# Linear attention and a silu feed-forward on one core: which queue issues the loads and the DMA transposes, in which order, and from which buffers

## The chip, the cores and the metric

The kernel runs on one core of a Trainium2 chip. The core has five engines with their own in-order instruction streams: PE (TensorE, matrix multiply into PSUM), DVE (VectorE), ACT (ScalarE), POOL (GpSimd) and SP (SyncE), and 16 DMA engines that move data. SP computes nothing; it issues transfers. Any stream that issues a transfer is held for the time of the issue, and an instruction that waits holds all that stand behind it in its stream. The metric is the device time in microseconds (us), the median of several runs.

## The reference

The inputs are q, k, v of shape (4 batches, 8 heads, 768 positions, 64), a decay `lam` per head, and two weights, (512, 2048) and (2048, 512), all float32. First comes linear attention with decay, in blocks of 64 positions, with a 64 x 64 state per batch and head:

```python
for b in range(nb):
    intra = (qb @ kb^T * Dmask) @ vb             # Dmask[i,j] = lam^(i-j) for i >= j, else 0
    inter = (qb * lam^(pos+1)) @ kv_state
    out[b] = intra + inter
    kv_state = lam^64 * kv_state + (kb * lam^(63-pos))^T @ vb
```

The heads of one position are then put side by side, which gives x with 3072 rows of 512, and the result is `silu(x @ w_in) @ w_out`, 3072 x 512 in float32.

## The kernel before, in words

**Tiling.** The 3072 rows are 24 chunks of 128 positions, six to a batch. Heads go in pairs: a pair's two 64-wide heads fill the 128 partitions. The decay is put into q and v by two tables (`tab`, from Ln and Exp of `lam` in `c_tab`, lines 235 to 246), so the mask is a plain 0/1 one. For each chunk:

- `prep_q` (L353, once for two chunks) multiplies q by its table into `qb` (L371, POOL; the first queries also on DVE) and transposes it to `qT`.
- `prep_k` (L411) casts K to bf16 into `kbd` (L424), block-diagonal over the pair, with zeros set once beforehand, and transposes it to `kT`.
- `prep_v` (L454) multiplies V by its table into `vs` (L468, POOL) and copies that block-diagonally into `vbd` (L475, DVE).
- `attn` (L483) makes scores `sc` (L536) and masks them into `ss` (L542), sums the output `op` from scores and state (L565), adds to the state `kv` in PSUM (L585) and copies the state out as bf16 `sbd` (L599, L601). The output becomes `x` (L615, L617).

For chunks 0 to 7 (`NPET = 8`) the transposes are done on PE into PSUM tiles of tag `o`, and copied out (L387 to L400, L435 to L443). From chunk 8 on they are DMA transposes from one SBUF tile into another, issued on SP's queue (L406 for q, L448 for k).

**Feed-forward.** Chunks are gathered into groups of 2, 2, 2, 2, 4, 4, 4, 4 (`GROUPS`). `ffn1` (L626) makes 128 rows of the hidden layer at a time into PSUM `h` (L633), and ACT applies silu into `g` (L640). `ffn2` (L646) sums 16 such pieces into PSUM `o` (L656) for each chunk; ACT or DVE copies it to `ob` (L666), and SP stores it (L673).

**Loads.** K and V of chunks 0 to 3 come as two transfers of 128 KB each (`load_kvh`, L285 and L288, buffers `kfh` and `vfh`). All later K and V come in segments of 4 to 8 blocks of 64 positions (`SEGS`), one transfer per head, so eight per segment and tensor (`load_seg`, L303, two buffers `kf`, two `vf`). q comes in 512 KB (`load_q`, L275, two buffers). The weights come in float32 (`load_w`, L324, five buffers `wt`) and are cast into their places (L335, L337). Everything is issued by SP, in the order in which the program lists the loads (lines 680 to 708).

**What sets the order of work.** Nothing is written down by hand. Each step is an `Op` with its possible engines and an assumed duration, what it depends on, and the buffers it takes and uses. `plan` (L46) simulates the engines: it takes again and again the operation that can start earliest, ties going to the lower priority number, and gives it its engine. A buffer tag has `SLOTS[tag]` buffers; an operation that takes a new one waits in the plan for all users of the one that it replaces, and buffers of a tag must be taken in order, but for tag `o`. `FREE` is when each engine is assumed to begin, `SEEN` the delay until others see a result. A transfer is assumed to begin 1.3 us after its issue or when DMA is free, to move `bytes / rate`, and to be seen 0.7 us later; no more than eight are under way. The loads are a chain, each after the one before. The instructions are then emitted in the order of the planned starts, so each engine's stream, SP's too, has the order of this simulation:

```python
def load(fn, nbytes, ndesc, rate, deps=(), alloc=(), uses=(), prio=None):      # L262
    o = add(fn, ("SP", max(420.0, 60 + 1.05 * ndesc)), ..., after=chain[-1:])
```

Up to 26 us (`WARM`) gaps of PE in the plan are filled with multiplications by zero (L737).

Of the kernel before, what the change touches and what calls it, by code (L numbers as in the profile page):

```python
# [42 lines left out]
FREE = {"PE": 900.0, "DVE": 2400.0, "ACT": 900.0, "POOL": 3300.0, "SP": 900.0}  # L43


def plan(ops, slots):  # L46
    free = dict(FREE)
    dma_free = 0.0
    landed = []
    given = {t: [] for t in slots}  # L50
    for i, op in enumerate(ops):
        op.n = i
    todo = list(ops)
    order = []
    while todo:
        best = None
        for op in todo:
            ready = op.at
            ok = True
            for d in op.after:  # L60
                if d.start is None:
                    ok = False
                    break
                ready = max(ready, d.start)
            if not ok:
                continue
            for d in op.deps:
                if d.start is None:
                    ok = False
                    break  # L70
                if d.seen > ready and not (len(op.opts) == 1 and d.eng == op.opts[0][0] == "PE"):
                    ready = d.seen
            if not ok:
                continue
            for b in op.alloc:
                if b.tag != "o" and b.idx != len(given[b.tag]):
                    ok = False
                    break
                k = len(given[b.tag]) - slots[b.tag]
                if k >= 0:  # L80
                    for u in given[b.tag][k].users:
                        if u.start is None:
                            ok = False
                            break
                        if u.seen > ready:
                            ready = u.seen
                if not ok:
                    break
            if not ok:
                continue  # L90
            if op.bytes and len(landed) >= 8:
                ready = max(ready, landed[-8])
            for e, dur in op.opts:
                s = max(free[e], ready)
                key = (s, op.prio, s + dur)
                if best is None or key < best[0]:
                    best = (key, op, e, s, dur)
        if best is None:
            for op in todo[:40]:
                print(op.n, op.fn.__qualname__, op.prio, [d.n for d in op.deps + op.after if d.start is None],  # L100
                      [(b.tag, b.idx, len(given[b.tag])) for b in op.alloc])
        assert best is not None, "no operation can go on"
        _, op, e, s, dur = best
        op.start, op.eng, op.end = s, e, s + dur
        free[e] = s + dur
        if op.bytes:
            t = max(op.end + 1300.0, dma_free)
            dma_free = t + op.bytes / op.rate
            op.seen = dma_free + 700.0
            landed.append(op.seen)  # L110
        else:
            op.seen = op.end + SEEN[e]
        for b in op.alloc:
            given[b.tag].append(b)
        todo.remove(op)
        order.append(op)
    order.sort(key=lambda o: (o.start, o.n))
    return order
# [19 lines left out]
def kernel(  # L138
# [23 lines left out]
    SLOTS = {"qf": 2, "qb": 2, "qT": 3, "kf": 2, "vf": 2, "kfh": 2, "vfh": 2, "kbd": 3, "kT": 3, "vs": 3, "vbd": 3,  # L162
             "ss": 3, "sbd": 3, "x": 3, "g": 24, "ob": 3, "wt": 5, "sc": 1, "op": 1, "kv": 1, "h": 3, "o": 2}
# [61 lines left out]
    nc.vector.memset(zk[0], 0.0)  # L225
    nc.vector.memset(zv[0], 0.0)
    nc.vector.memset(zs[0], 0.0)
    late_zero = [zk[1], zv[1], zs[1], zk[2], zv[2], zs[2]]
# [33 lines left out]
    def load(fn, nbytes, ndesc, rate, deps=(), alloc=(), uses=(), prio=None):  # L262
        nload[0] += 1
        p = nload[0] if prio is None else prio
        o = add(fn, ("SP", max(420.0, 60 + 1.05 * ndesc)), deps=deps, alloc=alloc, uses=uses,
                nbytes=nbytes, rate=rate, prio=p, after=chain[-1:])
        chain.append(o)
        return o

    def load_q(b, j):  # L270
        t = Buf("qf")

        def f():
            new(t, [128, H, 2, D], F32)
            nc.sync.dma_start(out=t.tile, in_=q[b, :, 256 * j:256 * j + 256, :].rearrange("h (s t) d -> s h t d", t=2))  # L275
        o = load(f, 524288, 1024, 330.0, alloc=[t])
        return t, [o]

    def load_kvh(src, tag, b, c):
# [7 lines left out]
        def f1():  # L287
            nc.sync.dma_start(out=t.tile[64:128], in_=r[1])  # L288
        a = load(f0, 131072, 256, 330.0, alloc=[t])
        z = load(f1, 131072, 256, 330.0, uses=[t])  # L290
        return t, [a, z]

    def load_seg(src, tag, b, c0, n):
        t = Buf(tag)
        last = []
        for hh in range(8):
# [7 lines left out]
            o = load(f, 64 * n * 256, 64 * n, 222.0, alloc=[t] if hh == 0 else [], uses=[] if hh == 0 else [t])  # L304
            last.append(o)
# [4 lines left out]
    def load_w(which, i, n):  # L310

        t = Buf("wt")
# [12 lines left out]
        o = load(f, 524288 * n, 512 if which == "in" else 256 * n, 386.0, alloc=[t])  # L325
# [27 lines left out]
    def prep_q(b, j, head):  # L353
# [9 lines left out]
        prep = []  # L363
        for i in range(nn):
            sl = slice(2 // nn * i, 2 // nn * (i + 1))

            def f(e, i=i, sl=sl):
                if i == 0:
                    new(tb, [128, 2, H, D], BF16)
                eng = nc.gpsimd if e == "POOL" else nc.vector  # L370
                eng.tensor_tensor(tb.tile[:, sl], tf.tile.rearrange("p h s d -> p s h d")[:, sl],  # L371
                                  tabq[:, j, sl, :, None].to_broadcast([128, 2 // nn, H, D]), op=AL.mult)
            opts = [("POOL", pool_ns(1024 // nn))] + ([("DVE", dve_ns(512))] if head else [])
            prep.append(add(f, opts, deps=list(o) + [o_tab], after=prep, alloc=[tb] if i == 0 else [],
                            uses=[tf] + ([tb] if i else []), prio=pr(c)))
        if c < NPET:
            ps = Buf("o")
            tr = []
            for i in range(nn):
                sl = range(2 // nn * i, 2 // nn * (i + 1))  # L380

                def ft(i=i, sl=sl):
                    if i == 0:
                        new(ps, [128, 2, NP, 128], BF16)
                    for s in sl:
                        for p in range(NP):
# [4 lines left out]
            for i in range(nn):  # L391
                sl = slice(2 // nn * i, 2 // nn * (i + 1))

                def fe(e, i=i, sl=sl):
                    if i == 0:
                        new(tq, [128, 2, NP, 128], BF16)
                    if e == "ACT":
                        nc.scalar.activation(tq.tile[:, sl], ps.tile[:, sl], AF.Copy)
                    else:
                        nc.vector.tensor_copy(tq.tile[:, sl], ps.tile[:, sl])  # L400
                z.append(add(fe, [("DVE", dve_ns(1024 // nn, 2)), ("ACT", act_ns(1024 // nn))], deps=[tr[i]], after=z,
                             alloc=[tq] if i == 0 else [], uses=[ps] + ([tq] if i else []), prio=pr(c)))
        else:
            def fx():
                new(tq, [128, 2, NP, 128], BF16)
                nc.sync.dma_start_transpose(out=tq.tile.rearrange("a s p b -> a (s p) b"),  # L406
                                            in_=tb.tile.rearrange("a s h d -> a (s h d)"))
            z = [add(fx, ("SP", 700.0), deps=prep, alloc=[tq], uses=[tb], nbytes=262144, rate=200.0, prio=-50)]
        qT[b, j] = (tq, z)

    def prep_k(c, src, src_ops, coff, head):  # L411
# [16 lines left out]
        if c < NPET:  # L428
            ps = Buf("o")
# [15 lines left out]
        else:  # L445
            def fx():
                new(tk, [128, 2, NP, 128], BF16)
                nc.sync.dma_start_transpose(out=tk.tile.rearrange("a s p b -> a (s p) b"),  # L448
                                            in_=kb.tile.rearrange("a s p h d -> a (s p h d)"))
            z = add(fx, ("SP", 700.0), deps=prep, alloc=[tk], uses=[kb], nbytes=262144, rate=200.0, prio=-50)  # L450
# [3 lines left out]
    def prep_v(c, src, src_ops, coff, head):  # L454
# [14 lines left out]
        a = add(f, [("POOL", pool_ns(512))] + ([("DVE", dve_ns(512))] if head else []), deps=list(src_ops) + [o_tab], alloc=[tv], uses=[src], prio=pr(c))  # L469
# [153 lines left out]
    gts = {}  # L623
    PF = 1000.0

    def ffn1(g, m):  # L626
        n = C * GROUPS[g]
        hb, gb = Buf("h"), Buf("g")
# [9 lines left out]
        def fe():  # L638
            new(gb, [128, n], BF16, padded=[128, 512])
            nc.scalar.activation(gb.tile, hb.tile, AF.Silu)  # L640
        z = add(fe, ("ACT", act_ns(n)), deps=[a], alloc=[gb], uses=[hb], prio=-30)
        gts[g, m] = (gb, z)
# [3 lines left out]
    def ffn2(g, mt):  # L646
        po = Buf("o")
        prev = None
        for kk in range(4):
            ms = range(4 * kk, 4 * kk + 4)  # L650

            def f(kk=kk, ms=ms):
                if kk == 0:
                    new(po, [128, DM], F32)
                for m in ms:
                    nc.tensor.matmul(po.tile, lhsT=gts[g, m][0].tile[:, mt * C:(mt + 1) * C], rhs=w_out_bf[:, m, :],  # L656
# [3 lines left out]
                       uses=([] if kk == 0 else [po]) + [gts[g, m][0] for m in ms], prio=PF + 100 * g + 20 + 4 * mt + kk)  # L660
# [13 lines left out]
        add(fd, ("SP", 420.0), deps=[z], uses=[bo], nbytes=262144, rate=386.0, prio=-40)  # L674
# [6 lines left out]
    loaded_q[0, 0] = load_q(0, 0)  # L681
# [8 lines left out]
    loaded_q[0, 1] = load_q(0, 1)  # L690
# [3 lines left out]
    for i in range(4, 8):  # L694
        load_w("in", i, 1)
    for i in range(0, 8, 2):
        load_w("out", i, 2)
    loaded_q[0, 2] = load_q(0, 2)
    for i, (b, c0, n) in enumerate(SEGS):
        seg_k[i] = load_seg(k, "kf", b, c0, n)  # L700
        seg_v[i] = load_seg(v, "vf", b, c0, n)
        for j in range(3):
            if (b, j) not in loaded_q and 4 * j + 4 <= c0 + n + 2:
                loaded_q[b, j] = load_q(b, j)
    for b in range(B):
# [4 lines left out]
    zero_ops = [add(lambda t=t: nc.gpsimd.memset(t, 0.0), ("POOL", 1100.0), prio=-70 + 20 * (i > 2)) for i, t in enumerate(late_zero)]  # L710
# [23 lines left out]
    for op in plan(ops, SLOTS):  # L734
# [6 lines left out]
        if "e" in op.fn.__code__.co_varnames[:op.fn.__code__.co_argcount]:  # L741
# [33 lines left out]
```

## Time and profile before

| | |
|---|---|
| median of 3 runs | 251.68 us (250.38 to 253.49) |
| the profiled execution's own time | 250.55 us |
| its span in the profile | 248.8 us |
| mean granted clock of PE | 0.977 |
| PE busy | 214.9 us, 86% |
| ACT, DVE, POOL busy | 119.4, 108.5, 52.7 us |
| bytes read from HBM, written | 27.27 MB, 6.29 MB |
| all bytes of the DMA queues | 40.15 MB, 161 GB/s over the span |
| first L633 (feed-forward) on PE | 19.75 us |
| last L565 (attention) on PE | 188.0 us |

How to read it: the span is cut into stages by what PE does. Until about 20 us it has the first two chunks' attention and zero multiplications; then feed-forward and attention alternate; from 190 us the last feed-forward groups alone are left, with PE never idle until the last copy and store. "Busy" of PE includes the zero multiplications (11.3 us). A wait "A <- B: 68.1, 5, 18.0" says that A waited for B 68.1 us in total, five times, 18.0 us at the longest; idle time of an engine that nobody waits for costs nothing. The queue of SP as an issuer is written SPq.

### The profile page before, as it was taken

Reading aid. Unit: us, or ns where it says so; the run is one execution under the profiler, and the core shown is the slowest. Engines: PE = TensorE matmul, PEld = TensorE weight load, DVE = VectorE, ACT = ScalarE, POOL = GpSimd, SP = SyncE. Lnnn points to the kernel's source line nnn. Section 1 sums busy time; section 2 is a strip of 40 time slices with the busy share of each in tenths; the row PEclk is TensorE's granted clock in tenths of the full one; section 3 lists DMA queues with packets and bytes.
Section 4 is the critical chain, followed back from the end, with each engine's and each line's share of the span. In section 5 each row is a group of like instructions: output and inputs, shape, how many; then the busy total and the mean of one; then the engine's idle time right before and its main releaser. Section 6 shows DMA issues by size and latency. Waiting matters only on the chain.

```text
span 248.8 us, 4537 instructions
## 1 busy us (share of the span) xinstructions
PE 214.9 (86%) x1781; PEld 126.3 (51%) x1781; DVE 108.5 (44%) x197; ACT 119.4 (48%) x230; POOL 52.7 (21%) x58
## 2 busy tenths in 40 slices
PE   6679899969599699566999896995899999999994
PEld 4477776735397386322455352443454444444441
DVE  4884852447286846594177247255740000000000
ACT  2369776723166287421685233654434751177310
POOL 7802100330320910180061005504300000000000
PEclk9999999997889999997999999999999999999999
DMA  5999999544698998699767989979442001210022
GB/s 143 243 281 251 358 383 328 140 125 91 178 243 190 251 216 154 127 285 211 148 161 162 167 192 237 217 156 191 80 122 84 0 0 45 84 42 0 5 82 84
DMA packets 94885, 40.15 MB, mean 161 GB/s; under 512 B 69264, under 2 KB 89744, under 8 KB 94864
## 3 DMA queue, kind: packets, MB, share of 16 engines
q1 hardware_dynamic: 94720, 39.86, 68.1%
q8 instruction: 14, 0.23, 0.4%
q14 instruction: 7, 0.06, 0.1%
q10 hardware_dynamic: 144, 0.00, 0.0%
HBM read 27.27 MB, written 6.29 MB: 135 GB/s over the span
## 4 chain that ended last, share of the span: by engine, by line
PE 48%; DMA 19%; SPq 15%; DVE 9%; issue 3%; POOL 2%; ACT 2%; POOLq 0%; DVEq 0%; ACTq 0%
PE h L633 22%; PE o L656 19%; SPq L303 10%; DMA qf<-in_q_dram 8%; DVE vbd L475 5%; DMA vf<-in_v_dram 3%; DMA wt<-in_moe_w_in_dram 3%; PE op L565 3%; DMA kfh<-in_k_dram 2%; DMA qT<-qb 2%; PE kv L737 2%; DVE sbd L601 1%; POOL vs L468 1%; DMA kf<-in_k_dram 1%; DVE ss L542 1%
## 5 line engine op out<-in xcount | busy, mean ns | idle before, releaser
L633 PE MATMUL h<-x,w_in_bf 128*128 128x256 bf16 (+1 forms) x512 | 92.8, 333 | 0.4 <-ACT g L640 0.4
L656 PE MATMUL o<-w_out_bf,g 128*128 128x512 bf16 x384 | 90.3, 383 | 0.0
L640 ACT ACTIVATE g<-h 128x256 bf16<-128x256 f32 (+1 forms) x128 | 62.0, 490 | 35.8 <-PE h L633 34.0
L633 PEld LDWEIGHTS <-w_in_bf 128*128 128x128 bf16 x512 | 48.9, 99 | 32.9 <-issue 2.2
L656 PEld LDWEIGHTS <-g 128*128 128x128 bf16 x384 | 35.7, 99 | 37.3 <-issue 1.1
L468 POOL TENSOR_TENSOR vs<-vf,tab 128x512 bf16<-128x512 f32 x20 | 20.8, 1062 | 86.4 <-DMA vf<-in_v_dram 68.1
L475 DVE COPY vbd<-vs 64x512 bf16<-64x512 bf16 x48 | 29.6, 617 | 19.5 <-POOL vs L468 18.8
L666 ACT ACTIVATE ob<-o 128x512 f32<-128x512 f32 x24 | 14.3, 597 | 44.6 <-PE o L656 43.5
L371 POOL TENSOR_TENSOR qb<-qf,tab 128x1024 bf16<-128x1024 f32 (+1 forms) x12 | 22.3, 1856 | 34.5 <-DMA qf<-in_q_dram 34.4
L585 PE MATMUL kv<-vs,kbd 128*128 128x64 bf16 x176 | 12.1, 196 | 17.9 <-POOL vs L468 8.9
L599 ACT ACTIVATE sbd<-kv 64x256 bf16<-64x256 f32 x42 | 15.8, 376 | 23.5 <-PE kv L585 18.9
L424 DVE CAST kbd<-kf 64x512 bf16<-64x512 f32 x40 | 19.4, 486 | 16.1 <-DMA kf<-in_k_dram 15.3
L585 PEld LDWEIGHTS <-kbd 128*128 128x128 bf16 x176 | 10.2, 100 | 26.3 <-issue 16.9
L542 DVE TENSOR_TENSOR ss<-sc,mask 128x512 bf16<-128x512 f32 x20 | 13.8, 691 | 16.0 <-PE sc L536 15.6
L601 DVE CAST sbd<-kv 64x256 bf16<-64x256 f32 x38 | 16.0, 422 | 7.9 <-PE kv L585 3.4
L565 PE MATMUL op<-ss,vbd 128*128 128x64 bf16 (+1 forms) x192 | 15.3, 198 | 1.3 <-DVE ss L542 1.0
L615 ACT ACTIVATE x<-op 128x512 bf16<-128x512 f32 x16 | 11.9, 746 | 8.5 <-PE op L565 8.4
L737 PE MATMUL kv<-zt 128*128 128x256 bf16 x69 | 11.3, 319 | 3.7 <-ACT sbd L599 2.1
L565 PE MATMUL op<-qT,sbd 128*128 128x64 bf16 (+1 forms) x160 | 14.4, 196 | 0.0
L565 PEld LDWEIGHTS <-vbd 128*128 128x128 bf16 x192 | 12.8, 99 | 2.5 <-DVE vbd L475 0.6
L565 PEld LDWEIGHTS <-sbd 128*128 128x128 bf16 x160 | 11.5, 99 | 2.7 <-issue 1.3
L536 PE MATMUL sc<-qT,kT 128*128 128x64 bf16 x160 | 7.9, 193 | 4.7 <-DMA kT<-kbd 3.0
(52 smaller groups left out, 94.5 us busy)
## 6 DMA issues: line engine op xcount, KB each, us to landing
qf<-in_q_dram SPq DMA_DIRECT2D x12, 512.0 KB, 5.2
out_dram<-ob SPq DMA_DIRECT2D x24, 256.0 KB, 2.4
wt<-in_moe_w_in_dram SPq DMA_DIRECT2D x8, 512.0 KB, 7.0
wt<-in_moe_w_out_dram SPq DMA_DIRECT2D x4, 1024.0 KB, 10.0
kf<-in_k_dram SPq DMA_DIRECT2D x32, 96.0 KB, 3.0
vf<-in_v_dram SPq DMA_DIRECT2D x32, 96.0 KB, 2.8
kfh<-in_k_dram SPq DMA_DIRECT2D x8, 128.0 KB, 5.6
vfh<-in_v_dram SPq DMA_DIRECT2D x8, 128.0 KB, 5.6
```

Of the source, the lines that this page charges most:

```text
L303: nc.sync.dma_start(out=t.tile[64 * two:64 * two + 64, :, p, :], in_=r)
L371: eng.tensor_tensor(tb.tile[:, sl], tf.tile.rearrange("p h s d -> p s h d")[:, sl], tabq[:, j, sl, :, None].to_broadcast([128, 2 // nn, H, ...
L424: nc.vector.tensor_copy(kb.tile[hs, :, :, h, :], i)
L468: eng.tensor_tensor(tv.tile, i, t[:, :, :, None].to_broadcast([128, 2, NP, D]), op=AL.mult)
L475: nc.vector.tensor_copy(vb.tile[hs, :, :, h, :], tv.tile[hs])
L542: nc.vector.tensor_tensor(sb.tile.rearrange("a s p b -> a (s p) b"), ps.tile.rearrange("a s p b -> a (s p) b"), mask1[:, None].rearrange(" ...
L565: nc.tensor.matmul(o_cols(p, sub), lhsT=l, rhs=r, start=not ovs["started"], stop=i == len(steps) - 1, skip_group_check=True)
L585: nc.tensor.matmul(kvp.tile[:, p, :], lhsT=kb.tile[:, s, p, :, :], rhs=tv.tile[:, s, p, :], start=st, stop=True, skip_group_check=True)
L601: nc.vector.tensor_copy(nb.tile[hs, :, h, :], kvp.tile[hs])
L633: nc.tensor.matmul(hb.tile, lhsT=w_in_bf[:, ko, m * 128:(m + 1) * 128], rhs=xt[g].tile[:, ko, :], start=(ko == 0), stop=(ko == 3))
L640: nc.scalar.activation(gb.tile, hb.tile, AF.Silu)
L656: nc.tensor.matmul(po.tile, lhsT=gts[g, m][0].tile[:, mt * C:(mt + 1) * C], rhs=w_out_bf[:, m, :], start=(m == 0), stop=(m == 15))
```

## The change

- **First loads.** The second halves of each `load_kvh` and of the first two q loads (heads 4 to 7) are issued by ACT, the first halves by SP. The two products of a head's `prep_q` are split by heads in place of by position parity, each waits for its own half, and both are on DVE.
- **Transposes.** Both DMA transposes are issued by ACT in place of SP. PE's transposes of chunks 0 to 7, which there were before, take PSUM tiles of tag `h` (three) in place of `o` (two).
- **Loads and buffers.** K and V segments and weights share seven buffers `big` (before: 2 `kf`, 2 `vf`, 5 `wt`, of the same size); q has four buffers in place of two. `SEGS` stays as it is. The last four `w_in` loads become two of 1 MB. The last two `w_out` loads come after the first segment, and each batch's q before the segments that need it.
- **g.** With 256 columns, two pieces of the hidden layer share one `g` buffer, so 24 buffers hold twice as many of them.
- **Zeroing.** The block-diagonal tiles are all zeroed on DVE; before, those of the second and third buffers were zeroed on POOL. V products of chunks 2 and 3 no longer may go to DVE.
- **The planner.** Assumed issue times are constants (620, 650, 660, 400, 560 ns; 1280 for a transpose), rates are lower, loads are planned no more than 5 us ahead of DMA once it is booked past 40 us, and after 60 us results are assumed to be seen 0.4 us later, transfers 3 us later.

```diff
-FREE = {"PE": 900.0, "DVE": 2400.0, "ACT": 900.0, "POOL": 3300.0, "SP": 900.0}
+FREE = {"PE": 900.0, "DVE": 2600.0, "ACT": 1200.0, "POOL": 5000.0, "SP": 800.0}
+LATE = 60000.0
+DEPTH = 5000.0
...
-                if b.tag != "o" and b.idx != len(given[b.tag]):
+                if b.tag not in ("o", "h") and b.idx != len(given[b.tag]):
...
+            if op.bytes and op.prio > 0.0 and dma_free > LATE - 20000.0:
+                ready = max(ready, dma_free - DEPTH)
...
+        if op.bytes and op.rate == 170.0:
+            dma_free = max(op.end + 1300.0, dma_free) + op.bytes / op.rate
+            op.seen = op.end + 2000.0 + 2.0 * op.bytes / op.rate
...
+            if op.start > LATE:
+                op.seen += 3000.0
         else:
-            op.seen = op.end + SEEN[e]
+            op.seen = op.end + SEEN[e] + (400.0 if op.start > LATE else 0.0)
...
-    SLOTS = {"qf": 2, ..., "kf": 2, "vf": 2, ..., "wt": 5, ...}
+    SLOTS = {"qf": 4, ..., "big": 7, ...}
...
-    def load(fn, nbytes, ndesc, rate, deps=(), alloc=(), uses=(), prio=None):
+    def load(fn, nbytes, issue, rate, alloc=(), uses=(), eng="SP"):
...
-        def f1():
-            nc.sync.dma_start(out=t.tile[64:128], in_=r[1])
+        def f1():
+            nc.scalar.dma_start(out=t.tile[64:128], in_=r[1])
...
-                nc.sync.dma_start_transpose(out=tq.tile.rearrange("a s p b -> a (s p) b"),
+                nc.scalar.dma_start_transpose(out=tq.tile.rearrange("a s p b -> a (s p) b"),
...
-            z = [add(fx, ("SP", 700.0), deps=prep, alloc=[tq], uses=[tb], nbytes=262144, rate=200.0, prio=-50)]
+            z = [add(fx, ("ACT", 1280.0), deps=prep, alloc=[tq], uses=[tb], nbytes=262144, rate=170.0, prio=-50)]
...
+        half = n == 256 and m % 2
+        gb = gts[g, m - 1][0] if half else Buf("g")
...
-    loaded_q[0, 0] = load_q(0, 0)
+    loaded_q[0, 0] = load_q(0, 0, ("SP", "ACT"))
...
-    for i in range(4, 8):
-        load_w("in", i, 1)
-    for i in range(0, 8, 2):
-        load_w("out", i, 2)
-    loaded_q[0, 2] = load_q(0, 2)
+    load_w("in", 4, 2)
+    load_w("in", 6, 2)
+    load_w("out", 0, 2)
+    load_w("out", 2, 2)
     for i, (b, c0, n) in enumerate(SEGS):
-        seg_k[i] = load_seg(k, "kf", b, c0, n)
-        seg_v[i] = load_seg(v, "vf", b, c0, n)
         for j in range(3):
-            if (b, j) not in loaded_q and 4 * j + 4 <= c0 + n + 2:
+            if 4 * j < c0 + n and (b, j) not in loaded_q:
                 loaded_q[b, j] = load_q(b, j)
+        seg_k[i] = load_seg(k, b, c0, n)
+        seg_v[i] = load_seg(v, b, c0, n)
+        if i == 0:
+            load_w("out", 4, 2)
+            load_w("out", 6, 2)
```

## The prediction

> **What bounds the kernel now.** I read the chain that ended last first, because engine shares alone (PE busy for 86% of the span) don't say what the other engines made PE wait for.
>
> ```profile
> PE 48%; DMA 19%; SPq 15%; DVE 9%; issue 3%; POOL 2%; ACT 2%; POOLq 0%; DVEq 0%; ACTq 0%
> ```
>
> Half of the chain is not PE. 15% of 248.8 us, 37 us, is SP's queue issuing transfers, and 19%, 47 us, is transfers on their way. So I went to the table by stage (the columns are the stretch, its length, busy us of PE, PE loads, DVE, ACT, POOL, then PE's granted clock, DMA share and GB/s).
>
> ```profile
> 20.00:50.00 30.00, 27.99 (x278) 21.51 (x276) 15.73 (x30) 22.43 (x46) 4.49 (x3) 1.00 1.00 293
> 50.00:80.00 30.00, 24.74 (x249) 16.97 (x246) 18.22 (x35) 12.71 (x29) 5.98 (x5) 0.89 0.71 158
> 80.00:110.00 30.00, 24.30 (x258) 16.01 (x256) 20.05 (x31) 14.33 (x33) 12.64 (x10) 1.00 0.97 206
> 110.00:140.00 30.00, 26.18 (x224) 13.39 (x222) 15.70 (x29) 16.30 (x32) 7.42 (x6) 0.94 0.86 173
> 140.00:165.00 25.00, 20.63 (x156) 10.15 (x155) 11.13 (x23) 10.03 (x18) 6.89 (x5) 1.00 0.93 205
> 165.00:190.00 25.00, 21.27 (x237) 11.92 (x236) 13.70 (x24) 10.51 (x21) 4.99 (x4) 1.00 0.61 127
> 190.00:248.80 58.80, 55.18 (x256) 24.84 (x254) 0.00 (x0) 24.48 (x41) 0.00 (x0) 0.99 0.11 41
> ```
>
> Three stages can be read off. From 20 to 50 us DMA is full (share 1.00) and PE nearly so. From 190 us on PE only works off the feed-forward groups that are left. Between, from 50 to 190 us, PE is idle for 5.3 + 5.7 + 3.8 + 4.4 + 3.7 = 22.9 us, and in three of its ten-us stretches the granted clock is 0.83 or 0.84: 7.36 + 7.38 + 6.72 = 21.5 us of PE work there that would take about 17.9 us at full clock, 3.6 us lost. So 26.5 us are to be had in the middle. Who ends the idle time? The view of waits says V and Q transfers, through POOL:
>
> ```profile
> POOL vs L468 <- DMA vf<-in_v_dram: 68.1, 5, 18.0
> POOL qb L371 <- DMA qf<-in_q_dram: 34.4, 9, 18.1
> ```
>
> And why do those land late? SP's own order of time (start, length, line):
>
> ```profile
> 33.04 12.08 SPq L303 DMA_DIRECT2D kf<-in_k_dram  x8
> ...
> 51.74 5.23 SPq L303 DMA_DIRECT2D kf<-in_k_dram  x8
> 57.01 6.35 SPq L303 DMA_DIRECT2D vf<-in_v_dram  x8
> ...
> 80.99 3.63 SPq L448 DMA_TRANSPOSE kT<-kbd  x2
> 84.67 2.65 SPq L303 DMA_DIRECT2D kf<-in_k_dram  x4
> ```
>
> Eight issues that normally take 5 us took 12 at 33 us, in the stage where DMA is full of weights. From there SP runs without a gap: between 49.1 and 180 us (131 us) its issues add up to 123 us: 100 of L303 are 69.9, 16 key transposes 29.0, 7 query transposes 11.1, 12 stores 7.2, 9 query loads 5.8. The V loads are late because they stand last in a full queue, not because they move slowly (median 2.8 us from issue to landing). DMA's share falls to 0.71 between 50 and 80 us: it is short of issues there, not of bandwidth.
>
> **The change part by part.** The sum is made against the profiled execution, 250.55 us (span 248.8 us and 1.75 us around it).
>
> *Transposes off SP.* All 24 come after 78 us, 23 of them before 180; these hold SP for 29.0 + 11.1 = 40.1 us, about 16 us of it waiting for their inputs (7.4 + 3.0 + 2.1 + 1.7 + 1.3 and less). SP's work from 49 to 180 us falls from 123 to 83 us. V and K loads can then be issued up to 40 us earlier by the end of the stage; SP stops being the late one.
>
> ```profile
> L448 SPq DMA_TRANSPOSE kT<-kbd x16: 1231/1274/2836, 78.2 to 177.9; - x16
> ```
>
> *The same transposes on ACT.* 24 issues by 1.28 us (median of the row) are 31 us on ACT's queue. ACT is busy 14.33 + 16.30 + 10.03 + 10.51 = 51.2 us between 80 and 190; with them 82 of 110 us, 75%. Behind each issue stand silu (L640), state copies (L599), x (L615) and output copies (L666). PE waits for silu when the three h buffers are full: at 512 columns one is filled in 0.86 us (the chain has eight matmuls of L633 in 1.73 us, 216 ns each, four to a buffer), so two spare buffers hide about 1.7 us, more than one issue of 1.28 us but less than two in a row or one that waits for its input. Bounds: nothing, if the spare buffers always hide them; 31 us, if each stops PE. I take 2.5 us, two of 24, since single issues are the common row.
>
> *A chunk's K and V before the last w_out.* `out` 4 and 6 (2.1 MB) now come behind the query load for chunks 4 and 5 and the first segment. At the 0.36 MB per us that the slices between 25 and 43 us moved (358, 383, 328 GB/s), these land about 5.8 us earlier; that also ends most of the 12.08 us that L303 spent stuck. Segment 0's V landed near 53.7 us (POOL's first L468), so near 47; the next ones, issue-bound, follow some 7 us earlier. The price: w_out rows 4 to 7 land about 6 us later than now (casts near 42 us), and the second half of group 0's FFN2, 16 matmuls by 216 ns = 3.5 us, and all of group 1's have to wait. PE can fill in FFN1 of group 1 and then of group 2, because the paired g buffers hold three 256-column groups in place of one and a half. That cover fails if x of chunks 4 and 5 isn't there by 45 us. Bounds 0 to 6 us; I take 2.
>
> *Larger shared buffers, four q buffers.* Seven "big" buffers serve weights and segments. They remove SP's buffer waits at the weights (2.3 + 1.2 + 1.0 + 0.7 us of L324) and let a third segment be under way. No separate gain: SP and DMA stay full until 45 us. If a buffer is released late, SP waits in front of stores and other loads; that can cost up to one segment's landing, 3.7 us.
>
> *The first loads on two queues.* Of the nine SP issues before the first weight (L275 to L288, about 0.62 us each) SP keeps five: the weights start 4 x 0.62 = 2.5 us earlier. DMA is at 0.79 in the first 10 us and above 1 from 10 to 30 us, so at most what is idle comes back: 0.21 x 10 = 2 us. Against it, five issues, 3.1 us, go to ACT, whose Ln at 3.42 us begins the decay table that the first products need; behind the table load of 1.28 us they can put it off by a us. I take a gain of 0.5; bounds 2 gained and 1 lost.
>
> *Zeroing on DVE, query halves by heads, chunks 2 and 3's V on POOL.* A kbd or vbd memset takes 0.485 us on DVE (L225), 1.07 on POOL; sbd 0.27. Four and one of them, 2.2 us, move into DVE's first 6 us, where it waits 1.24 + 0.52 us. Uncovered, 0.5 to 1.3 us go to the first kbd. Against that, the cast at 9.79 us took 1.58 us beside POOL's memset, 0.42 us elsewhere. Two half products on DVE are 2 x 0.69 = 1.38 us against one of 1.54 on POOL. All even, plus or minus 1 us.
>
> *Transposes in PSUM's h, not o.* Twelve tiles of chunks 0 to 7. They stop holding back FFN2's o and begin to hold back FFN1's h; PE waited 0.4 us for silu in all. Even, plus or minus 1 us.
>
> *The planner's numbers* (issue 0.66 us for a seg load where the formula gave 0.42 to 0.60, 0.56 for a store, loads no more than 5 us ahead of DMA) have no instruction of their own. They match the rows (0.62, 0.56), so an in-order queue should less often hold an instruction whose input is late.
>
> **Sum.** Of the middle's 26.5 us I take two thirds as recovered, 17.7: the SP wait is behind nearly all of it, but the serial end of a chunk (vs, vbd, state) stays, with DVE's vbd copies at 2 to 3 us beside POOL's work for 0.29 alone. 250.55 - 17.7 - 0.5 + 2.5 + 2.0 = 236.9 us. The profiled execution lies 1.1 us under the median 251.68, so 238.0 for a median. (The three runs are 1.2% apart, so 2% is about what can be told from no change.)
>
> A page of the Trainium skill speaks against this: "DMA: Bandwidth & Descriptors", section "Issuing engines are not separate DMA queues", says that DMAs begun on several engines share the same 16 DMA engines and save only the issue time, usually small beside the transfer. Here eight issues of 0.62 us stand beside a landing of 2.8 us, so it isn't small in this trace; were the rule right, only the reordering would be left, and the time would be the second case below.
>
> **The rivals.**
>
> *Transfers, not issues (chance 0.16).* DMA's share is 0.97, 0.86, 0.93 between 80 and 165 us. If it is full there, freeing SP moves nothing, and only 50 to 80 us gains: 5.3 + 2.4 us of clock, less ACT's 2.5: 250.55 - 5.2 = 245.3, near 246.5 as a median, with 242 to 252 around it. For it: 0.97. Against it: only 158 to 206 GB/s move, where 293 moved between 20 and 50 us.
>
> *ACT becomes the in-order bound (0.17, slower).* A transpose on ACT waits for its input with silu behind it, as SP did for 16 us. If each of the 24 stops PE for its 1.28 us and those 16 us are added, 47 us stand against the gain of 18.2 and a cost of 2: 281; at half of that 258, which I take as its time (257 to 270). It decides once ACT has more than about 20 us of such stops. For it: ACT at 75% and silu the heaviest row on it. Against: h buffers, and ACT starts at 51 of 110 us.
>
> *The middle fills completely (0.12).* All 26.5 us come back: 250.55 - 26.5 - 0.5 + 2 = 225.6, a median near 226.5.
>
> The forecast itself has 0.55, from 232 to 244. Range 226 to 252, which leaves out the ACT case and little else. Faster by over 2% (under 246.6): 0.55 + 0.12 and 0.05 of the transfer case, 0.72; within 2%: the rest of that, 0.11; slower 0.17.
>
> **What would show it.** Right: SPq's share of the chain under 6%; PE idle between 50 and 190 us of some 9 us; granted clock near 1 between 50 and 70 us; first POOL L468 of segment 0 before 48 us; SP with gaps. The pure feed-forward end gets longer than 55 us, since attention ends earlier. Wrong: "PE h <- ACT g" waits of many us (ACT case); POOL's waits for V still long while SP has gaps (transfer case); PE idle between 38 and 50 us for w_out above 4 us.

## The result

The changed kernel takes 263.30 us (median of 4 runs, 262.00 to 265.11), the kernel before 251.03 us beside it: a ratio of 1.048, 95% interval 1.037 to 1.059. It is slower by 5%, where the forecast was 5% faster. The profile is of the 265.11 us execution, and its span is 263.4 us. In all that follows medians are of all runs, while a ratio compares those runs of each kernel that lie near its fastest, since some executions are some per cent slower whatever the kernel.

The chain that ended last, of the kernel after:

```profile
PE 45%; DMA 31%; DVE 13%; POOL 2%; issue 2%; SPq 2%; ACT 2%; ACTq 1%; POOLq 0%; DVEq 0%
PE o L676 22%; PE h L651 17%; DMA kT<-kbd 9%; DMA big<-in_v_dram 8%; DVE vbd L491 7%; DMA vfh<-in_v_dram 5%; DMA kfh<-in_k_dram 3%; PE op L581 3%; DMA qT<-qb 3%; POOL vs L484 2%; DMA big<-in_k_dram 2%; SPq L321 2%; DVE kbd L440 1%; DVE sbd L617 1%; DVE w_out_bf L354 1%
```

SP's issuing has gone from 15% to 2%, as predicted, and the time has gone up all the same: transfers on their way now hold 31%, with key transposes and V loads in turn. The table by stage (stretch, its length, busy us of PE, PE loads, DVE, ACT, POOL, PE's granted clock, DMA share, GB/s), first for the kernel before, then for the kernel after:

```profile
0.00:50.00 50.00, 42.60 (x414) 32.99 (x415) 29.72 (x58) 31.01 (x59) 14.75 (x29) 1.00 0.99 266
50.00:190.00 140.00, 117.13 (x1117) 68.44 (x1114) 78.80 (x140) 63.89 (x131) 37.93 (x29) 0.96 0.82 175
```

```profile
0.00:50.00 50.00, 37.81 (x350) 30.21 (x351) 28.95 (x59) 23.71 (x46) 11.48 (x26) 0.90 0.93 246
50.00:190.00 140.00, 116.19 (x1056) 68.19 (x1054) 80.45 (x141) 57.59 (x121) 33.13 (x24) 0.95 0.86 174
190.00:263.40 73.40, 67.58 (x392) 31.73 (x389) 8.40 (x15) 29.12 (x51) 3.09 (x3) 1.00 0.14 49
```

Two losses are to be seen. In the first 50 us PE is busy for 4.8 us less, and at a granted clock of 0.90 for 1.00 (the last section has two executions of one kernel that differ as much). In the middle it is idle for 23.8 us, where 22.9 were to shrink to 9. At 190 us there are 392 matmuls left where there were 256, and attention (L581) ends at 206.8 us for 188.0.

Who holds SP? Its waits, kernel after, all of the span (us in total, times, longest):

```profile
SPq L321 <- DMA kT<-kbd: 21.2, 8, 4.1
SPq L321 <- DMA qT<-qb: 20.2, 6, 5.4
```

L321 is the plain load of a K or V segment. It uses nothing of a transpose, and before the change it had no such wait. The built program tells why. Each transfer raises one of eight completion semaphores (DMAHW0 to 7), which are handed out in turn over all transfers of SP and ACT alike, and each waits until the transfer that had the same semaphore, the eighth before it, has landed (where an earlier wait of its stream has not covered that). From the lists of SP and ACT about 73 us into the run (some lines left out):

```
SP   L321 DMACopy big<-in_k_dram [waits DMAHW7]
ACT  L422 DmaTranspose qT<-qb    [waits DMAHW0, Pool]
SP   L321 DMACopy big<-in_k_dram [waits DMAHW1]
SP   L321 DMACopy big<-in_k_dram [waits DMAHW2]
...
SP   L321 DMACopy big<-in_k_dram [waits DMAHW7]
SP   L321 DMACopy big<-in_k_dram [waits DMAHW0]   <- the transpose above
```

So a load stands behind a transpose that is issued by another engine, in that engine's own order. As long as SP issued all but the one small load of the decay, the eighth before had been issued by the same stream. The trace agrees: the transpose above lands at 82.78 us, and the load that waits for its semaphore is issued at 82.79. What it does is seen in SP's order of time and ACT's, kernel after (start, length, line):

```profile
77.40 5.98 SPq L321 DMA_DIRECT2D big<-in_k_dram  x3
```

```profile
76.02 1.53 ACTq L422 DMA_TRANSPOSE qT<-qb  x1
78.78 1.57 ACTq L422 DMA_TRANSPOSE qT<-qb  x1
86.56 5.64 ACTq L464 DMA_TRANSPOSE kT<-kbd  x3
92.25 0.94 ACT L659 ACTIVATE g<-h 128x256 bf16<-128x256 f32 x3 [7.58 <-DMA kT<-kbd]
```

Three issues, 0.61, 1.15 and 0.59 us long, take 6 us on SP, 3.6 of them the wait for the transpose. On ACT three transposes hold the queue for 5.6 us; ACT computes nothing for 7.6 us, and PE waits 3.7 us of that for silu.

The first loads meet the same rule. ACT's order of time, kernel after:

```profile
3.67 0.61 ACTq L306 DMA_DIRECT2D vfh<-in_v_dram  x1
5.84 0.61 ACTq L306 DMA_DIRECT2D kfh<-in_k_dram  x1
6.50 0.21 ACT L247 ACTIVATE ll<-lam_sb 128x8 f32<-128x8 f32 x1 [3.96 <-DMA qf<-in_q_dram]
```

Ln, the start of the decay table, needs only the decay, which lands at 3.65 us (before, Ln ran at 3.42), but it stands behind two issues that wait for semaphores and runs at 6.50. The first feed-forward matmul comes at 22.8 us for 19.8.

### The profile page after: what moved, and what is told of

Same layout as the page of the kernel before. It is cut to its first block, busy times and chain, and to the rows that moved or that the text cites. A ratio compares the mean times of both kernels' runs of the same rounds, so it can differ in the third digit from the quotient of the medians.

```text
span 263.4 us, 4547 instructions
## 1 busy us (share of the span) xinstructions
PE 221.6 (84%) x1794; PEld 130.1 (49%) x1794; DVE 117.8 (45%) x215; ACT 110.4 (42%) x217; POOL 47.7 (18%) x53
## 4 chain that ended last, share of the span: by engine, by line
PE 45%; DMA 31%; DVE 13%; POOL 2%; issue 2%; SPq 2%; ACT 2%; ACTq 1%; POOLq 0%; DVEq 0%
PE o L676 22%; PE h L651 17%; DMA kT<-kbd 9%; DMA big<-in_v_dram 8%; DVE vbd L491 7%; DMA vfh<-in_v_dram 5%; DMA kfh<-in_k_dram 3%; PE op L581 3%; DMA qT<-qb 3%; POOL vs L484 2%; DMA big<-in_k_dram 2%; SPq L321 2%; DVE kbd L440 1%; DVE sbd L617 1%; DVE w_out_bf L354 1%
## 5 line engine op out<-in xcount | busy, mean ns | idle before, releaser
L651 PE MATMUL h<-x,w_in_bf 128*128 128x256 bf16 (+1 forms) x512 | 98.5, 339 | 7.5 <-ACT g L659 4.5
L491 DVE COPY vbd<-vs 64x512 bf16<-64x512 bf16 x48 | 29.8, 621 | 23.9 <-POOL vs L484 23.2
L484 POOL TENSOR_TENSOR vs<-big,tab 128x512 bf16<-128x512 f32 x20 | 20.6, 1056 | 104.2 <-DMA big<-in_v_dram 33.3
L686 ACT ACTIVATE ob<-o 128x512 f32<-128x512 f32 x20 | 11.9, 597 | 34.4 <-PE o L676 32.5
L389 POOL TENSOR_TENSOR qb<-qf,tab 128x1024 bf16<-128x1024 f32 x10 | 19.7, 1973 | 18.2 <-DMA qf<-in_q_dram 18.2
L581 PE MATMUL op<-ss,vbd 128*128 128x64 bf16 (+1 forms) x192 | 17.7, 203 | 5.6 <-DVE ss L558 4.5
L440 DVE CAST kbd<-big 64x512 bf16<-64x512 f32 x40 | 17.5, 439 | 5.3 <-DMA big<-in_k_dram 4.3
L581 PE MATMUL op<-qT,sbd 128*128 128x64 bf16 (+1 forms) x160 | 16.4, 198 | 1.0 <-ACT x L631 0.5
L760 PE MATMUL kv<-zt 128*128 128x256 bf16 x82 | 14.0, 315 | 3.8 <-ACT sbd L615 2.6
L581 PEld LDWEIGHTS <-vbd 128*128 128x128 bf16 x192 | 13.6, 101 | 5.5 <-DVE vbd L491 2.6
L581 PEld LDWEIGHTS <-sbd 128*128 128x128 bf16 x160 | 12.1, 100 | 5.4 <-issue 3.8
L633 DVE CAST x<-op 128x512 bf16<-128x512 f32 x15 | 10.9, 729 | 7.3 <-PE op L581 7.2
L760 PEld LDWEIGHTS <-zt 128*128 128x128 bf16 x82 | 8.9, 113 | 5.9 <-issue 3.1
```

Of the source, the lines that this page charges most:

```text
L389: eng.tensor_tensor(tb.tile[:, :, hs], tf.tile.rearrange("p h s d -> p s h d")[:, :, hs], tabq[:, j, :, hs, None].to_broadcast([128, 2, hn ...
L440: nc.vector.tensor_copy(kb.tile[hs, :, :, h, :], i)
L484: eng.tensor_tensor(tv.tile, i, t[:, :, :, None].to_broadcast([128, 2, NP, D]), op=AL.mult)
L491: nc.vector.tensor_copy(vb.tile[hs, :, :, h, :], tv.tile[hs])
L581: nc.tensor.matmul(o_cols(p, sub), lhsT=l, rhs=r, start=not ovs["started"], stop=i == len(steps) - 1, skip_group_check=True)
L651: nc.tensor.matmul(hb.tile, lhsT=w_in_bf[:, ko, m * 128:(m + 1) * 128], rhs=xt[g].tile[:, ko, :], start=(ko == 0), stop=(ko == 3))
```

## The experiments

All ratios are to the kernel before, measured on the same chip.

| run | median us | ratio, 95% interval |
|---|---|---|
| the change | 263.30 | 1.048, 1.037 to 1.059 |
| a_trans_sp | 248.43 | 0.985, 0.978 to 0.992 |
| a_head_sp | 259.04 | 1.025, 1.016 to 1.034 |
| a_both_sp | 243.42 | 0.965, 0.958 to 0.973 |
| b_trans_act, again as b_trans_act2 | 255.40, 256.16 | 1.001, 0.995 to 1.007 (the second) |
| b_head_act | 254.07 | 1.014, 1.006 to 1.021 |
| a_tab_first | 251.91 | 0.998, 0.992 to 1.004 |
| a_head_sp_deep | 251.00 | 0.996, 0.992 to 1.000 |
| a_both_wout | 244.53 | 0.973, 0.962 to 0.985 |
| a_both_pe | 244.89 | 0.975, 0.967 to 0.983 |
| a_both_nolate | 245.70 | 0.972, 0.964 to 0.981 |
| a_both_g1 | 244.60 | 0.970, 0.962 to 0.977 |
| a_both_psum | 240.69 | 0.954, 0.948 to 0.960 |
| a_both_alt | 244.89 | 0.971, 0.958 to 0.983 |
| a_psum_q1 | 240.02 | 0.956, 0.950 to 0.963 |

### Undoing the two moves, one by one and together

```diff
-                nc.scalar.dma_start_transpose(out=tk.tile...          # a_trans_sp, L422 and L464
+                nc.sync.dma_start_transpose(out=tk.tile...
-            z = add(fx, ("ACT", 1280.0), ...
+            z = add(fx, ("SP", 1280.0), ...
```

> The kernel after, with both DMA transposes issued by SP again (1280 ns of SP in the plan); everything else as after. Theory A, coupling of the queues: the program gives all transfers eight completion semaphores in turn, whichever queue issues them, so a load on SP waits for the transfer eight before it, and when that is a transpose that ACT has not come to yet, SP stands still (38 us of such waits after 72 us). Then the waits of L321 for kT and qT fall from 38 us to under 5, and the time falls by 6 to 12 us, to 251 to 257. Theory B, the first 40 us: nearly all of the loss is made by the first loads on ACT, which hold the decay table (Ln at 6.50 us for 3.42) and the V of chunks 2 and 3: then no more than 3 us come back, 260 to 263. Theory C, the transposes are slower from a second queue (landing 4.5 us for 3.5): landing returns to 3.5 us, and the time falls by some 24 x 1 us at most, less what is hidden: 255 to 260, with SP's waits falling only in that proportion.

```diff
-            nc.scalar.dma_start(out=t.tile[64:128], in_=r[1])         # a_head_sp
+            nc.sync.dma_start(out=t.tile[64:128], in_=r[1])
-    loaded_q[0, 0] = load_q(0, 0, ("SP", "ACT"))
+    loaded_q[0, 0] = load_q(0, 0, ("SP", "SP"))
```

> The kernel after, with the second halves of the first K, V and q loads issued by SP again (still as halves); transposes stay on ACT. Theory B: Ln back near 3.4 us, the first feed-forward matmul some 3 us earlier, and most of the loss is gone: 252 to 256. Theory A: the head gains 3 to 5 us, which the middle keeps only in part: 258 to 262, with SP's waits for the transposes as before this edit (30 us or more).

a_both_sp has both edits.

> Both undone: no transfer of ACT but the decay's. What is left of the change is order, buffers, halves and the planner's numbers. Theory A with B's head loss: 246 to 252, at or a little under the kernel before, since segment 0 still comes before the last w_out. If the order of the loads or the planner's numbers were what makes it slower, it stays above 256.

Transposes back on SP: 263.3 to 248.4, 14.9 us, more than any theory gave, and no wait of SP for kT or qT is left. First loads back on SP: 4.3 us alone, 5.0 when the transposes are back too. Both: 19.9 us, about the sum. So the two moves cost 20 us, and all else in the change gains 8 (3.5%) over the kernel before. Theory B's main claim falls: the head is a quarter of it. Theory C does not carry the 14.9 us alone. The transposes' median landing was 4.5 (keys) and 4.4 us (queries) in the change, 3.7 for both in a_trans_sp, so 24 of them would cost 18 us if nothing hid any of it; but C had SP's waits shrink only in that proportion, and they are gone. A share of it is not excluded. The stages of a_both_sp:

```profile
0.00:50.00 50.00, 42.37 (x433) 34.23 (x435) 29.54 (x61) 31.82 (x63) 11.60 (x26) 1.00 0.88 242
50.00:190.00 140.00, 125.22 (x1116) 71.52 (x1136) 76.53 (x141) 67.72 (x137) 36.13 (x27) 0.98 0.84 185
```

The head is back (42.37 us at full clock), and the middle's idle time is 14.8 us, 8.1 less than before the change.

That the transposes on ACT cost 14.9 us is shown by undoing them. How the cost reaches PE is less clear, since two routes are open: SP's loads behind ACT's transposes, and ACT's own work behind them. PE's waits from 50 to 190 us name both, first in the change, then in a_trans_sp:

```profile
PE kv L601 <- POOL vs L484: 7.9, 3, 3.3
PE h L651 <- ACT g L659: 4.3, 2, 3.7
```

```profile
PE sc L552 <- DMA kT<-kbd: 8.6, 4, 5.1
```

V's products (`vs`), whose loads stand behind SP's waits, cost PE 7.9 us in the change and none in a_trans_sp. ACT's results cost it 8.6 us in the change (`g` 4.3, `sbd` 2.2, `x` 2.1) and 2.7 in a_trans_sp (`sbd` 1.4, `x` 1.3). In return PE waits 8.6 us for kT there and none in the change. No run divides the 14.9 us between the two routes.

### The transposes on ACT in the kernel before

```diff
-                nc.sync.dma_start_transpose(...                       # L406, L448; ("SP", 700.0) -> ("ACT", 1280.0)
+                nc.scalar.dma_start_transpose(...
```

> The kernel before with one part alone: both DMA transposes issued by ACT (1280 ns of ACT in the plan). Theory A: loads of SP begin to wait for kT and qT, 20 to 40 us in all where there were none, and the time rises by 4 to 10 us, to 255 to 261. Theory B: no change, 249 to 254. My prediction's step: SP is freed of 40 us and the time falls, to 240 to 246.

> The kernel before with both transposes on ACT again, timed longer, because its four runs lay between 249.6 and 256.7. If transposes on ACT cost something in every order of loads, 253 to 257. If they cost only where loads are planned just in time, no loss to be told: 249 to 254.

SP now waits for transposes here too, kernel b_trans_act2, 20 to 190 us:

```profile
SPq L303 <- DMA kT<-kbd: 15.1, 7, 3.8
SPq L303 <- DMA qT<-qb: 6.4, 4, 2.9
SPq L673 <- DMA kT<-kbd: 3.9, 3, 2.0
SPq L275 <- DMA kT<-kbd: 3.6, 2, 3.1
```

29 us in all, yet no loss is to be told: 1.001. Its 12 runs lie between 250.0 and 259.9 us, wider than the 249.2 to 254.6 of the kernel before, and why is open. The edit moves the planned order of the head too (first feed-forward matmul at 23.2 us for 19.8), so the ratio is of the whole order and not of the transposes alone. My step, a fall to 240 to 246, is refuted by this run alone: SP got rid of 40 us of transposes and got 29 us of waits for them. But the same move that costs nothing here costs 15 us in the change. Several things differ between the two kernels; how far ahead the loads are planned is the one that was tested.

### Loads further ahead, transposes on ACT

```diff
-DEPTH = 5000.0                                                       # on top of a_head_sp
+DEPTH = 20000.0
```

> Transposes on ACT, first loads on SP, and loads planned up to 20 us ahead of DMA in place of 5. Coupling made dear by loading just in time: with loads further ahead, SP's waits for kT and qT (44 us in the kernel with 5 us) still occur but PE feels them less: 250 to 255. If the cost is ACT's own (silu and copies standing behind transposes that wait), the depth doesn't matter: 257 to 261.

From 1.025 to 0.996: 8.0 us by the medians, 7 by the ratios. SP's waits, in a_head_sp and then in a_head_sp_deep:

```profile
SPq L321 <- DMA kT<-kbd: 25.8, 8, 5.0
SPq L321 <- DMA qT<-qb: 18.0, 6, 4.6
```

```profile
SPq L321 <- DMA kT<-kbd: 21.7, 8, 5.3
SPq L321 <- DMA qT<-qb: 14.9, 4, 4.8
SPq L293 <- DMA kT<-kbd: 6.6, 2, 5.5
```

43.8 us of waits against 43.2: the same, and 7 to 8 us less time. So the waits are dearer when loads are planned 5 us ahead than when they are planned up to 20 us ahead. The rival in its plain form, that the cost is ACT's own and the depth doesn't matter, is refuted. The two routes are not told apart, though: with the depth PE's waits between 50 and 190 us fall on both, for ACT's results from 9.3 to 3.5 us and for V's products from 6.9 to 3.4. And 7.6 us to a_both_sp stay, half of the 15.6 that the transposes cost a_head_sp, which this doesn't divide further.

> All issues on SP; the planner without its late rules (no 5 us limit on loads ahead, no later sight of results after 60 us). My prediction gave these numbers no price. If the gain of 8 us over the kernel before comes from the better modelled order, some of it goes: 246 to 251. If loads simply run further ahead and the stores wait little: 241 to 245.

This one sets `LATE` beyond the end on top of a_both_sp, so neither the 5 us limit nor the later sight of results applies. With the transposes on SP it makes no difference that can be told (0.972 and 0.965, intervals overlap), which fits the depth mattering only where the transposes are on ACT.

### The first loads

```diff
-    o_tab = add(c_tab, ("ACT", 2600.0), at=3300.0, prio=-100)        # a_tab_first, on top of a_trans_sp
+    o_tab = add(c_tab, ("ACT", 2600.0), at=1900.0, prio=-300)
```

> Transposes on SP, first halves' partners on ACT as in the change, but the decay table (Ln, Exp) put in ACT's order before the V, and second K issue, which wait for completion semaphores. If the head loses because the table stands behind those two issues, Ln goes from 6.4 to about 3.5 us and 2 to 4 us of the 5 us between 248.4 and 243.4 come back: 244 to 247. If the loss is in the later halves (chunks 2 and 3, standing between silu and copies on ACT), the table is early but the time stays at 247 to 249.

A miss: the table's Ln ran at 3.66 us and the time rose, 0.998 for 0.985. ACT's order of time in a_tab_first shows the wait in its new place:

```profile
3.66 0.21 ACT L247 ACTIVATE ll<-lam_sb 128x8 f32<-128x8 f32 x1 [1.13 <-DMA lam_sb<-in_lam_dram]
7.87 0.61 ACTq L306 DMA_DIRECT2D vfh<-in_v_dram  x1
```

V's second half, issued at 3.5 us in a_trans_sp, goes out at 7.9, right after its first half, the eighth transfer before it, has landed at 7.84. The first feed-forward matmul slips from 24.3 to 27.8 us. The table is early, and V pays in its place.

> The kernel before with one part alone: second halves of the first K and V issued by ACT (q stays whole on SP). If the head's 5 us come from issues that stand on ACT between its table, copies and silu and wait there for completion semaphores, the first feed-forward matmul is 1 to 4 us later than 19.8 us and the time is 252 to 257. If they come from q's halves alone (twice the transfers for the same bytes), it stays at 250 to 253.

The edit is the first one of a_head_sp reversed, in the kernel before: K's and V's second halves on ACT, q whole on SP. 1.014 (1.006 to 1.021), so ACT's issues cost some 3 us by themselves; the first feed-forward matmul comes 0.4 us later, less than expected, but PE is idle for 4.2 us between 20 and 50 us, where it was 2.0.

> All issues on SP, PE transposes in o, and the first two q loads whole again (two transfers fewer for eight semaphores). If fewer transfers help the head, 238 to 240.5; if the halves let DVE start sooner, 241 to 243.

This is a_both_psum, below, with both q loads whole: 0.956 against 0.954, no difference. q's halves by themselves cost nothing.

### Where the gain of the rest comes from

```diff
-        if i == 0:                                                   # a_both_wout
-            load_w("out", 4, 2)
-            load_w("out", 6, 2)                                       # moved ahead of the segments
```

> All issues on SP, and the last two w_out loads again before the first segment, as in the kernel before. My prediction's step: segment 0 lands some 6 us later, the price of the late w_out (2 us) comes back; together 245 to 248 for the 243.4 us with the changed order. If the order is worth nothing: 242 to 245.

```diff
-        half = n == 256 and m % 2                                    # a_both_g1
+        half = 0
```

> All issues on SP; one piece of the hidden layer to a g buffer again, so 24 buffers hold one and a half groups of 256 columns. If PE's lower idle time from 50 to 80 us (2.8 us for 5.3 before) rests on FFN1 running ahead, it rises by 2 to 4 us: 245 to 248. If not: 242 to 245.

Neither can be told from a_both_sp (0.973 and 0.970 against 0.965, intervals overlap). The gain that my prediction looked for in segment 0's earlier landing is not to be seen.

```diff
-                if b.tag not in ("o", "h") and b.idx != len(given[b.tag]):   # a_both_psum
+                if b.tag not in ("o",) and b.idx != len(given[b.tag]):
...
-            ps = Buf("h")                                            # in prep_q and prep_k
+            ps = Buf("o")
```

> All issues on SP; the PE transposes of chunks 0 to 7 in PSUM tiles of o, taken as in the kernel before. My prediction: even, plus or minus 1 us: 242 to 245. A rival: the two o buffers hold back FFN2 in the first 70 us, 246 to 250.

0.954 against 0.965: some 2.7 us faster, though the two intervals just overlap. If anything, giving the transposes h buffers, and letting h buffers be taken out of order, was a loss. This and a_psum_q1, 4.5% under the kernel before, are the best versions that the runs found.

```diff
-NPET = 8                                                             # a_both_pe
+NPET = 24
```

> All issues on SP, and PE transposes for all 24 chunks, so there is no DMA transpose. It takes 40 us from SP and 6.3 MB from DMA, and adds 24 x 8 PE transposes (0.45 us per 8, 11 us of PE) and 24 copies of 0.7 to 1.0 us to DVE and ACT. If SP's issue time or DMA's share is what starves PE in the middle, that returns more than 11 us of the 18 us of idle PE: 236 to 243. If the waits are of the serial chain at a chunk's end (vs, vbd, state), PE's 11 us are simply added: 248 to 256.

```diff
-        if c < NPET:                                                 # a_both_alt
+        if c < NPET or c // 2 % 2 == 0:
```

> All issues on SP; of chunks 8 to 23 every second pair is transposed on PE, the others by DMA: half of the kernel with no DMA transposes (244.9, PE idle in the middle almost gone but 11 us of PE work added). PE work rises by 5 us, SP is freed of 20 us. If SP's issue time is what starves PE, idle falls by more than those 5 us: 237 to 242. If it is the serial end of a chunk: 244 to 249.

Both come out at 244.9 us, outside the hoped-for ranges; for a_both_alt that is the range of its rival, the serial end of a chunk (244 to 249), for a_both_pe it is in neither range. Without any DMA transpose, a_both_pe's middle is:

```profile
50.00:190.00 140.00, 131.24 (x1314) 81.11 (x1335) 82.34 (x156) 77.41 (x149) 36.92 (x29) 0.99 0.58 144
```

Idle 8.8 us for 14.8, attention ends at 162.7 us for 191.5 in a_both_sp, and SP now waits 45.1 us for output copies between 20 and 190 us. That fits attention having waited for the transposes' time on SP and DMA. But only 6 us of idle time come back, and PE's busy time rises from 214.8 to 224.4 us, which takes the gain back. With half of the chunks (a_both_alt) attention ends at 171.0 us and the time is the same.

## Why the prediction was wrong

**The step that failed** is "Transposes off SP": "SP's work from 49 to 180 us falls from 123 to 83 us. V and K loads can then be issued up to 40 us earlier". The issue time fell as counted (SPq 2% of the chain). But the loads were not free to go: 41 us of waits for kT and qT took its place, and the 17.7 us were not recovered by this route at all (1.001 in the kernel before). What the prediction lacks is that a load waits for the eighth transfer before it, whichever queue has it. One row of the kernel before had it: K's loads need no query, and yet one of them waits for a query load, the eighth before it (SP's waits up to 50 us):

```profile
SPq L303 <- DMA qf<-in_q_dram: 0.9, 1, 0.9
```

The row that I did read, eight L303 issues in 12.08 us at 33 us, is another matter. But for that 0.9 us they hardly wait; single issues last long, the first of them 5.2 us without waiting for any semaphore (shortest, median and longest issue in ns):

```profile
L303 SPq DMA_DIRECT2D kf<-in_k_dram x56: 595/622/5197, 33.0 to 161.3; - x56
```

What holds such an issue stays open; DMA's share is 1.00 there. The prediction had the changed order end most of it, and that is wrong too: the first eight L321 issues of the change take 12.24 us, from 27.1 us on.

Four of the signs that I had named for being right came true all the same (SPq at 2% of the chain, a granted clock of 1.00 between 50 and 70 us, segment 0's V before 48 us, gaps on SP): they tell that SP issues less, not that it is free.

**"The same transposes on ACT"**, 2.5 us taken, bounds 0 to 31: the move measured 14.9 us in the change. The mechanism I gave, silu and the copies held back until PE starves, is a part of it: PE waited 4.5 us for silu in all, and 8.6 us for all of ACT's results in the middle, 2.7 in a_trans_sp.

```profile
PE h L651 <- ACT g L659: 4.5, 3, 3.7
```

I listed "PE h <- ACT g" waits of many us as the mark of the slower rival. 4.5 us is little of that, so the rival, at 257 to 270 us, gave about the right time partly by luck: it had ACT's queue as the bound, and the runs show loads of SP that stand behind ACT's transposes beside it. Which of the two carries more stays open.

**"The first loads on two queues"**, a gain of 0.5 with a loss of 1 as the bound: 5 us lost (a_both_sp against a_trans_sp). The bound considered that ACT's issues, 3.1 us of them, put off the table by about a us; it did not consider that they wait, and Ln came 3.1 us late.

**"A chunk's K and V before the last w_out"**: segment 0's V was first used at 46.7 us, where I said "near 47", and 53.7 before. That landing was right; but its worth is not to be told from nothing (a_both_wout).

**The middle's idle time** was to fall from 22.9 to "some 9 us". It rose to 23.8, and even where the moves are undone (a_both_sp) 14.8 are left. One reading behind the part that was to stay is off as well: the vbd copies of "2 to 3 us" are rows of two copies, set against 0.29 us for one; the longest single copy took 2.0. That a_both_sp, 243.4 us, lies within the forecast's 232 to 244 is luck: it has no relief of SP in it, and it is the rest of the change that gained the 8 us. Which item of it carries most stays open: load order, g buffers and the late planner rules, undone alone, each gave no difference that can be told, and the shared buffers were not tried alone.

**The planner's numbers**: "an in-order queue should less often hold an instruction whose input is late" did not hold in the change. With the limit of 5 us ahead the waits cost 7 to 8 us more than with one of 20 us.

The rule of the Trainium skill that I had weighed ("DMA: Bandwidth & Descriptors", section "Issuing engines are not separate DMA queues": only the issue time is saved) was nearer than I was. In the kernel before not even that came back: SP got rid of 40 us of issue and waiting, and the time stayed the same (1.001).

## What to carry to other kernels

Before moving transfers to a second issuing engine, look at what each issue waits for. In these programs eight completion semaphores are handed out in turn over both queues, so the eighth transfer before must have landed, and one that stands in the order of a busy compute engine stops loads that have nothing to do with it. Moved transposes also hold back what their new engine computes. Tell a wait in front of an issue, which the view of waits names, from an issue that itself lasts several times its usual length, as the 5.2 us one did without a wait. And if queues are coupled, loads need lead: much the same waits, 43 to 44 us, cost 7 to 8 us less when the loads were planned up to 20 us ahead.

## What was not expected of the hardware

A DMA transpose of 128 x 1024 bf16 landed in 3.3 to 4.3 us (medians of the runs) when SP issued it with the loads, and in 3.7 to 4.8 us from ACT's queue beside them. It holds the issuing queue for 1.25 to 1.34 us on either engine (medians; one row of b_trans_act2 has 1.45 and one of a_psum_q1 1.63), twice as long as a load's 0.62 us. PE's granted clock in the first 20 us was 1.00 in a_both_sp and 0.83 in the change, whose first feed-forward matmul comes 4 us later; but two profiled executions of one and the same kernel, b_trans_act and b_trans_act2, have 0.83 and 1.00 there. So the lower clock of the change's head is not shown to come from the change.
